# One set of raw token places for two groups, a half step with its transposes inside a product, and the last weight made in the last stage

## The chip, the core and the metric

The kernel runs on one core of one Trainium2 chip. A core has TensorE (PE, matrix products into PSUM, with its weight loads PEld beside them), VectorE (DVE), ScalarE (ACT), GpSimd (POOL) and SyncE (SP, which here issues most of the transfers). Each engine works through its own queue in order, and engines wait for each other by semaphores. The metric is the device time of one execution, in microseconds; the time of a kernel is the median of its runs.

## The reference

Three stages follow each other, all on 2304 tokens of 512 numbers:

```python
# 1. attention with a cumulative bias, 4 batches x 8 heads x 576 x 64
scores = scale * q @ k.T;  cum = cumsum(max(s, 0))
attn = softmax(where(causal, -1e9, scores + min(-(cum_i - cum_j), 0)))
x = attn @ v                               # 2304 x 512
# 2. mixture of 8 experts, each token to its best one
logits = x @ w_gate + modality_bias[modality_id];  e = argmax(logits)
x = prob[e] * (relu(x @ w1[e]) @ w2[e])    # F = 1024
# 3. gated projection, d_ff = 1536
out = (sigmoid(x @ w_gate2) * (x @ w_val)) @ w_out
```

The weights of stage 3 arrive as 64-bit numbers. The kernel makes 32-bit ones of them itself.

## The kernel before

**Order of work.** Everything is emitted by one program in one hand-made order, and each engine executes its part of it in that order. Attention runs a written period of steps over 16 pairs of heads. Between its steps `tick` takes one entry at a time from the router's queue `q` (an entry `None` lets a tick pass), and each batch of 576 tokens puts its routing steps there (`batch`, L622): the copy of the modality bias into the ninth column of the logits `lg` (POOL, L642), four empty ticks, their sum (L644), maximum, one-hot `oh` (L649), the entry `ranks` (small matmuls `rp`, L656 and L658, whose result is added into R at L653), the exponential, and the scatter of token numbers into a table. `lg` has two buffers, for batches of even and odd number.

**Expert stage.** When attention ends, `early` runs the first two slots of 256 tokens, 16 units; a unit is one eighth of the hidden size of one slot. It calls `main(u)` after each unit, which calls `router.pump(PUMPS[min(u, 3)])`: nine entries of the queue at unit 0, none at units 1 and 2, fourteen at each unit from 3 on. Unit 0's own products have already been emitted in attention; after `main(0)` come the products of unit 1. At unit 10 the table of tokens is transposed (`numbers`).

Then `run` (L1230) goes over units 16 to 71. In a unit, `mm1` makes twelve matmuls of 128x256, ScalarE writes the relu hH, VectorE the rest hL, and `mm2` of the unit before makes twelve more from hH and hL. After the unit `step(u)` emits what `todo` holds for it, and `aheads` splits the weights three units ahead (ScalarE `w`, then VectorE or POOL, L937 and L940) and loads the raw weights of the next slot. Unit numbers in `todo` are counted from 72 on: `put(-28, ...)` is unit 44.

After unit 71 come eight half steps (two half slots of 128 tokens, four steps each, `half`, L1129). A step transposes the hidden values of the step before (`half_t`, two matmuls L1111 and the VectorE copy hT, L1113), makes the first product (eight matmuls, L1134), has ScalarE write its relu, and then makes the second product of the step before (sixteen matmuls, L1122). `finish`, the last `mm2` of the slots, stands after the first half step.

**Filler work of the expert stage.** `Decode.stages` makes one piece of a 64-bit weight into 32 bits in four tasks: `near` (POOL, L877), `far` (VectorE, L881), `word` (ScalarE, L885) and `tail` (VectorE, L890), which also issues the next load. `last_weight` (L1290) does this for w_out, twelve pieces of 128x512 from unit 17 on, two units apart, and stores the results in DRAM as `wo32`. The eight pieces of the first gate and value weights (128x256 each) follow from unit 45 on, two units apart. `sums` (L1312) makes the seven sums of a token group that the fast product of stage 3 needs, in 18 tasks of 128x768: seven casts on ScalarE (L1317), seven rests (L1318) and four sums (L1319) on VectorE. Group 0 is loaded at unit 65 into four raw places `raws` and made at units 68 to 73, three tasks a unit. Group 1 has four raw places of its own (`raws1`), is loaded at unit 72 and made in units 74 to 79.

**Projection.** `Moe2.run` (L1662) goes over 36 units of seven slots. A slot is one product of six 128x384 matmuls per half (`product`, L1376); ScalarE takes a snapshot of a bank between two products into it (L1391), VectorE adds (L1403, L1410), ScalarE takes the sigmoid (L1405). Here too `todo` holds filler tasks by slot: group 2's sums up to slot 24, the pieces of the next weights (36 of them) in the slots from 12 on, and near the end the load of `wo32`. After that come the products with w_out.

The lines that order the filler work:

```python
for k, stages in enumerate(glu.last_weight(pool(wo_ctx, "dec", side="right", reuse_waits="tile"))):
    for i, task in enumerate(stages):
        put(2 * k + i - 55, [task])
...
put(-28, [wo_ctx.close, open_xs, glu.dec.load, glu.dec.load])
...
        put(2 * k + i - 27, [task])
...
put(-7, [lambda: glu.load_x(0, raws), lambda: glu.room_x(0, keep[0])])
```

Of the kernel before, what the change touches and what calls it, by code (L numbers as in the profile page):

```python
# [500 lines left out]
TROWS, PUMPS = 96, (9, 0, 0, 14)  # L501
# [5 lines left out]
class Router:  # L507
# [114 lines left out]
    def batch(self, b, xr, lg):  # L622
# [12 lines left out]
        tb = self.tb.rearrange("p (b t) e -> p b t e", t=5)[:, b]  # L635
# [36 lines left out]
        q.append(lambda: V.tensor_tensor(L, L, bc(mx), ALU.subtract))  # L672
        q.append(ranks)
# [174 lines left out]
class Decode:  # L848
# [7 lines left out]
    def __init__(self, tc, pool, n, srcs, bufs=2):  # L856
        self.nc, self.pool, self.srcs, self.size, self.bufs = tc.nc, pool, srcs, n, bufs
        self.raw, self.n, self.i = {}, 0, 0

    def load(self):  # L860

        if self.n < len(self.srcs):
            src = self.srcs[self.n]
            c, w = src.shape[1:]
            t = self.raw[self.n] = self.pool.tile([128, 8 * self.size], U8, tag="dr", name="dr", bufs=self.bufs)
# [3 lines left out]
    def stages(self, dst, then=None):  # L869

        nc, V, o, i, n = self.nc, self.nc.vector, {}, self.i, self.size
# [3 lines left out]
        def near():  # L875
            o["n"] = self.pool.tile([128, n], I8, tag="dn", name="dn", bufs=2)
            nc.gpsimd.tensor_scalar(o["n"], top(), 56.0, -56.0, ALU.min, ALU.max)  # L877

        def far():
            o["d"] = self.pool.tile([128, n], I8, tag="dd", name="dd", bufs=2)  # L880
# [17 lines left out]
class Moe:  # L898
    def __init__(self, tc, raw, ps, acc, router, w1, w2, x, x2, ids2, ident):
# [4 lines left out]
        self.prev, self.hprev, self.pend, self.ready = None, None, [], False  # L904
# [211 lines left out]
    def half_mm2(self, s, k, t):  # L1116
        nc = self.nc
        if k == 0:
            self.y[s] = [self.ps.tile([128, 512], F32, tag="tr", name="yh", bufs=BT)]
        for dc in range(4):  # L1120
# [5 lines left out]
        if k == 3:  # L1126
# [103 lines left out]
    def run(self, step):  # L1230
# [17 lines left out]
        ready = self.half_t(*self.hprev)  # L1248
        self.hprev = None
        self.half_mm2(*ready)  # L1250
# [7 lines left out]
class Moe2:  # L1258
# [10 lines left out]
    def __init__(self, tc, moe, x2, ids2, wg, wv, wo, out, hd, keep, rp, wo32):  # L1269
# [8 lines left out]
        self.dec = Decode(tc, keep, 256, srcs)  # L1278
# [11 lines left out]
    def last_weight(self, pool):  # L1290

        dec = Decode(self.tc, pool, 512, [self.wo[128 * f : 128 * f + 128, 3:].rearrange("(c p) b -> p c b", c=1) for f in range(12)], 3)
        for _ in range(3):
            dec.load()
        new = lambda: pool.tile([128, 512], F32, tag="dt", name="dt", bufs=2)
        return [dec.stages(new, lambda t, f=f: self.nc.sync.dma_start(self.wo32[128 * f : 128 * f + 128, :], t)) for f in range(12)]
# [365 lines left out]
    def run(self, ctx, rest):  # L1662
# [26 lines left out]
        spread(at(12, 0), at(15, 0), self.rows())  # L1689
        free = 0  # L1690
# [73 lines left out]
def kernel(ctx, tc, q, k, v, s, modality_id, moe_w_gate, modality_bias, w1, w2, wg, wv, wo, out):  # L1764
# [10 lines left out]
    with tc.manual_schedule():  # L1775
        ident = cp.tile([128, 128], F32, name="ident")
        make_identity(nc, ident)
        ps_ctx, at_ctx, mo_ctx, ea_ctx, mw_ctx, ex_ctx, xs_ctx, wo_ctx, x1_ctx = (ExitStack() for _ in range(9))
# [44 lines left out]
        def main(u):  # L1823
            if u >= 0:
                router.pump(PUMPS[min(u, 3)])
# [13 lines left out]
        todo, last, xs, raws, x1, raws1 = {}, 8 * MAIN, [], [], [], []  # L1839
# [99 lines left out]
```

## Time and profile before

| | us |
|---|---|
| median of three runs | 933.51 (931.78 to 933.62) |
| the profiled execution | 931.2 |
| its span, first to last instruction | 929.3 |
| TensorE busy | 890.6 (96%) |
| VectorE busy | 687.5 (74%) |
| ScalarE busy | 547.2 (59%) |
| POOL busy | 395.8 (43%) |
| granted TensorE clock, mean | 0.992 |

The span falls into attention (0 to about 250 us), the expert stage (to about 478), the half steps (to about 511) and the projection. Times of single instructions are counted from the start of the span. A matmul on full 32-bit operands appears as two records: the four of a half step's first product as eight, the eight of its second product as sixteen. Matmuls are pipelined, and their records overlap. Idle time is put down to the engine whose event came last before the start.

### The profile page before, as it was taken

How to read it: one execution, taken by the hardware profiler on the slowest of the kernel's cores; microseconds unless marked ns; L12 is line 12 of the kernel's file. 1: busy time of each engine (PE TensorE's matmuls, PEld its weight loads, DVE VectorE, ACT ScalarE, POOL GpSimd, SP SyncE). 2: the span in 40 equal slices, each digit the busy share in tenths (PEclk: the TensorE clock that was granted, in tenths of full speed). 3: DMA queues.
4: the chain of work that ended last, by engine and by line, in shares of the span. 5: the costliest groups of instructions: out<-in, count | busy, mean ns of one | idle time of the engine just before them, and what ended most of it. 6: DMA issues, size and time to landing. Idle time of an engine off the chain costs nothing. (4 is left out here: it accounts for less than half of the span.)

```text
span 929.3 us, 18666 instructions
## 1 busy us (share of the span) xinstructions
PE 890.6 (96%) x6261; PEld 856.7 (92%) x6261; DVE 687.5 (74%) x1549; ACT 547.2 (59%) x1282; POOL 395.8 (43%) x626
## 2 busy tenths in 40 slices
PE   7999999999889998999999999999999999999996
PEld 6898899898789998999998999999999998889996
DVE  5899999999765688867667766767575747868770
ACT  5999899898633656666544545354535345454440
POOL 7988889898822676776620001010000000111111
PEclk8999999999999999999999999999999999999998
DMA  6667659676314458523566422424242308573501
GB/s 170 155 146 177 142 94 141 154 146 225 97 22 80 143 176 262 193 92 92 178 211 215 114 81 80 139 78 136 74 139 68 116 18 300 153 225 110 170 35 45
DMA packets 163866, 125.29 MB, mean 135 GB/s; under 512 B 86737, under 2 KB 147692, under 8 KB 163254
## 3 DMA queue, kind: packets, MB, share of 16 engines
q1 hardware_dynamic: 158566, 112.44, 43.2%
q0 software_dynamic: 3984, 11.32, 4.3%
q8 instruction: 50, 0.82, 0.4%
q14 instruction: 50, 0.41, 0.2%
q10 hardware_dynamic: 1216, 0.30, 0.1%
HBM read 115.95 MB, written 33.23 MB: 161 GB/s over the span
## 5 line engine op out<-in xcount | busy, mean ns | idle before, releaser
L1382 PE MATMUL X<-a,set 128*128 128x384 f32 x864 | 164.1, 337 | 1.9 <-ACT u L1391 0.9
L1382 PEld LDWEIGHTS X<-a,set 128*128 128x128 f32 x864 | 151.7, 188 | 3.8 <-ACT u L1391 1.9
L877 POOL TENSOR_SCALAR dn<-dr 128x256 int8<-128x256 int8 (+1 forms) x60 | 34.4, 573 | 249.0 <-DMA dr<-in_moe_w_val_dram 91.3
L940 POOL TENSOR_TENSOR w<-raw,w 128x512 fp32r<-128x512 f32 x56 | 80.3, 1444 | 45.9 <-ACT w L937 43.6
L1519 POOL DMA_INDIRECT out_dram<-oy,row x18 | 20.2, 1120 | 167.5 <-ACT oy L1543 91.4
L175 POOL TENSOR_SCALAR bias<-cumB,cumT 128x576 f32<-128x576 f32 (+4 forms) x155 | 82.9, 537 | 19.3 <-DVE nm L294 18.3
L1004 PE MATMUL ph<-xT,w 128*128 128x256 f32 x672 | 88.6, 280 | 0.0
L1004 PEld LDWEIGHTS ph<-xT,w 128*128 128x128 f32 x672 | 82.4, 188 | 0.0
L1382 PE MATMUL Y<-a,set 128*128 128x384 f32 x432 | 81.5, 336 | 0.0
L303 ACT ACTIVATE P<-P,nm 128x576 f32<-128x576 f32 (+3 forms) x128 | 79.6, 628 | 0.6 <-DVE nm L294 0.6
L338 DVE TENSOR_TENSOR PL<-pt,PH 128x512 fp32r<-128x512 f32 (+1 forms) x128 | 76.9, 630 | 3.1 <-ACT PH L331 2.6
L1382 PEld LDWEIGHTS Y<-a,set 128*128 128x128 f32 x432 | 76.0, 188 | 0.1
L294 DVE CUSTOM_DVE_ANT_0 P<-sb,bias 128x320 f32<-128x320 f32 (+3 forms) x128 | 67.3, 550 | 6.4 <-PE sb L285 4.8
L1391 ACT COPY u<-X 128x384 f32<-128x384 f32 x72 | 34.5, 480 | 61.1 <-PE X L1382 61.0
L331 ACT CAST PH<-pt 128x512 fp32r<-128x512 f32 (+1 forms) x128 | 64.7, 551 | 5.8 <-PE pt L322 4.7
L322 PE MATMUL pt<-ident,P 128*128 128x128 f32 x448 | 64.1, 277 | 2.8 <-DVE QL L241 1.0
L1008 ACT ACTIVATE hH<-ph 128x256 fp32r<-128x256 f32 x72 | 27.7, 384 | 62.3 <-PE ph L1004 56.4
L940 DVE TENSOR_TENSOR w<-raw,w 128x512 fp32r<-128x512 f32 x56 | 54.7, 976 | 12.1 <-ACT w L937 11.4
L937 ACT CAST w<-raw 128x512 fp32r<-128x512 f32 x112 | 63.6, 619 | 0.0
L285 PE MATMUL sb<-KT,QH 128*128 128x288 f32 (+3 forms) x192 | 56.6, 319 | 4.7 <-DVE nm L294 4.2
L322 PEld LDWEIGHTS pt<-ident,P 128*128 128x128 f32 x448 | 51.6, 142 | 7.8 <-ACT P L303 3.2
L1317 ACT CAST hf<-hp 128x768 fp32r<-128x768 f32 x42 | 34.1, 835 | 38.9 <-DVE hp L1319 35.2
(317 smaller groups left out, 2393.2 us busy)
## 6 DMA issues: line engine op xcount, KB each, us to landing
raw<-in_moe_w_dram SPq DMA_DIRECT2D x80, 512.0 KB
h<-sg SPq DMA_DIRECT2D x72, 192.0 KB
cumB<-cum_d SPq DMA_DIRECT2D x32, 288.0 KB
hp<-h SPq DMA_DIRECT2D x24, 384.0 KB
qraw<-in_q_dram SPq DMA_DIRECT2D x58, 128.0 KB
dr<-in_moe_w_out_dram SPq DMA_DIRECT2D x12, 511.6 KB
dr<-in_moe_w_gate_dram SPq DMA_DIRECT2D x24, 255.2 KB
dr<-in_moe_w_val_dram SPq DMA_DIRECT2D x24, 255.2 KB
```

What stands on the lines that cost most here:

```text
L175: (nc.vector if n in FILLB else nc.gpsimd).tensor_scalar(res[i][:rows], cumB[:rows, :m], -1.0, self.cumT[:rows, i, n : n + 1], ALU.mult, A ...
L285: nc.tensor.matmul(self.sb[:rows, o : o + c1 - c0], X[:, T0[i] : T0[i] + rows], h["KT"][:, c0:c1], start=j == 0, stop=j == 1)
L294: nc.vector.tensor_tensor_reduce(out=pt[:rows, :m], in0=self.sb[:rows, o : o + m], in1=self.bias_t[n][i][:rows], op0=ALU.add, op1=ALU.min, ...
L303: nc.scalar.activation(h["P"][i][:rows, : T0[i] + rows], h["P"][i][:rows, : T0[i] + rows], AF.Exp, bias=h["nm", i][:rows], scale=-1.0, acc ...
L322: nc.tensor.transpose(pt[:, c : c + 128], h["P"][i][:, T0[j] : T0[j] + 128], self.ident)
L331: self.nc.scalar.copy(t[:, :z], pt[:, :z])
L338: self.nc.vector.tensor_tensor(t[:, :z], pt[:, :z], h["H"][u][:, :z].bitcast(F32), ALU.subtract)
L937: nc.scalar.copy(v, src)
L940: (eng or nc.vector).tensor_tensor(v, src, h.bitcast(F32), ALU.subtract)
L1004: nc.tensor.matmul(ph, w[:, 128 * dc : 128 * dc + 128], x[:, dc], start=k == 0, stop=k == 11)
L1382: self.nc.tensor.matmul(bank, w[:, c], a[:, h, c], start=first and k == 0, stop=k == 5, skip_group_check=True)
L1391: self.nc.scalar.copy(t, self.o[u, "X"])
```

## The change

Four things change together.

- The router's bias copy becomes `bias_in(b)`. It is made for the first two batches at set-up, and for batch b + 2 right after the sum of batch b. The four empty ticks ahead of the sum go. At unit 0 `pump` takes up to fourteen entries but stops ahead of the last batch's `ranks`; at units 1 and 2 it takes none, from unit 3 on fourteen.
- A half step transposes its own hidden values, after six of the eight matmuls (twelve of sixteen records) of the second product of the step before (`part=0`); the last two (`part=1`) follow the transposes. `half_end` then needs no transposes. In step 0 there is no second product yet, and the transposes follow the first product at once.
- w_out is made in the projection: 24 pieces of 128x256 instead of twelve of 128x512, 26/3 slots apart from slot 31 on, in places that group 2's raw values have left. The first gate and value weights take the room: their eight pieces are made from unit 24 on, four units apart.
- Group 0 is loaded at unit 54 and made one task at a time in units 56 to 70. Group 1 is loaded at unit 71 into the same raw places and made in units 73 to 80, two or three tasks a unit; the second set of places goes.

```diff
-TROWS, PUMPS = 96, (9, 0, 0, 14)
+TROWS, PUMP, RANKS = 96, 14, 3
+        for b in range(2):
+            self.bias_in(b)
+
+    def bias_in(self, b):
+        self.nc.gpsimd.tensor_copy(self.lg[b % 2][:, :, :, 8], self.tb.rearrange("p (b t) e -> p b t e", t=5)[:, b])
...
-        q.append(lambda: nc.gpsimd.tensor_copy(lg[:, :, :, 8], tb))
-        self.space(4)
         q.append(lambda: V.tensor_reduce(L.unsqueeze(3), lg, axis=AX.X, op=ALU.add))
+        if b + 2 < self.B:
+            q.append(lambda: self.bias_in(b + 2))
...
+        if b == self.B - 1:
+            self.last_ranks = ranks
         q.append(ranks)
...
-    def pump(self, n):
+    def pump(self, u):
         self.q = [f for f in self.q if f]
-        while self.q and n:
+        n = 0 if 0 < u < RANKS else PUMP
+        while self.q and n and (u or self.q[0] is not self.last_ranks):
...
     def half(self, s, k):
         nc = self.nc
-        ready = self.half_t(*self.hprev) if self.hprev else None
+        ready = self.hready
...
         if ready:
-            self.half_mm2(*ready)
-        self.hprev = (s, k, h)
+            self.half_mm2(*ready, part=0)
+        self.hready = self.half_t(s, k, h)
+        if ready:
+            self.half_mm2(*ready, part=1)

     def half_end(self):
-        self.half_mm2(*self.half_t(*self.hprev))
-        self.hprev = None
+        self.half_mm2(*self.hready)
+        self.hready = None
...
-    def last_weight(self, pool):
+    def last_weight(self):
...
+        raw = [self.ap.tile([128, 3072], U8, tag=f"xs{i}", name=f"dx{i}", bufs=1) for i in range(3)]
+        top = self.rp.tile([128, 4096], U8, tag="raw2_3", name="dx3", bufs=1)
+        dr = [raw[0][:, 0:2048], raw[1][:, 0:2048], top[:, 0:2048], top[:, 2048:4096]]
...
+        at = [(128 * f, 256 * l) for f in range(12) for l in range(2)]
...
+        def last_weight():
+            for k, stages in enumerate(self.last_weight()):
+                for i, task in enumerate(stages):
+                    put(at(4, 3) + 26 * k // 3 + i, [task])
+
+        put(at(3, 5), [last_weight])
...
-        for k, stages in enumerate(glu.last_weight(pool(wo_ctx, "dec", side="right", reuse_waits="tile"))):
-            for i, task in enumerate(stages):
-                put(2 * k + i - 55, [task])
...
-    put(-28, [wo_ctx.close, open_xs, glu.dec.load, glu.dec.load])
+    put(-49, [open_xs, glu.dec.load, glu.dec.load])
...
-            put(2 * k + i - 27, [task])
+            put(4 * k + i - 48, [task])
...
-    put(-7, [lambda: glu.load_x(0, raws), lambda: glu.room_x(0, keep[0])])
+    put(-18, [lambda: glu.load_x(0, raws), lambda: glu.room_x(0, keep[0])])
...
-        for k in range(6):
-            put(k - 4, x[3 * k : 3 * k + 3])
+        for k in range(18):
+            put(k * 5 // 6 - 16, [x[k]])
...
-        x, cuts = glu.x_tasks(1, raws1), (0, 3, 7, 9, 12, 15, 18, 18)
+        x, cuts = glu.x_tasks(1, raws), (0, 2, 4, 6, 9, 11, 13, 16, 18)
...
+    put(-1, [lambda: glu.load_x(1, raws)])
+    put(0, [later])
```

## Rows read from the trace of the kernel before

**Rows 1.** Waits of TensorE, whole span: line waited for, us in total, times, longest.

```profile
PE rp L656 <- DVE oh L649: 4.5, 1, 4.5
...
PE sb L1024 <- DVE hL L1009: 3.7, 4, 1.5
PE yh L1122 <- DVE hT L1113: 3.4, 3, 1.3
...
PE y L1024 <- DVE hL L1009: 1.9, 4, 0.9
```

**Rows 2.** Stretches: length, busy us (instructions) of each engine, clock, DMA share, GB/s.

```profile
320.00:383.00 63.00, 57.81 (x482) 56.39 (x481) 53.67 (x64) 38.12 (x78) 46.43 (x38) 1.00 0.68 221
383.00:430.00 47.00, 46.76 (x402) 46.56 (x402) 35.84 (x51) 30.11 (x65) 34.19 (x30) 1.00 0.29 92
...
478.00:512.00 34.00, 30.39 (x213) 27.81 (x211) 21.47 (x33) 13.66 (x26) 0.00 (x0) 1.00 0.59 195
512.00:545.00 33.00, 31.33 (x173) 29.96 (x174) 24.66 (x43) 19.15 (x39) 2.31 (x4) 1.00 0.39 113
545.00:775.00 230.00, 230.00 (x1316) 229.77 (x1316) 149.62 (x326) 105.83 (x235) 16.09 (x34) 1.00 0.30 99
```

**Rows 3.** TensorE in order of time, 252 to 265 us: start, us, line, shapes.

```profile
252.99 1.04 PE L988 MATMUL mtr<-ident,xg 128*128 128x128 f32 x8
258.50 0.20 PE L656 MATMUL rp<-oh,tri 128*128 128x48 bf16 x1 [4.48 <-DVE oh L649]
...
258.67 2.86 PE L1004 MATMUL ph<-xT,ew 128*128 128x256 f32 x12
...
263.12 1.60 PE L1004 MATMUL ph<-xT,ew 128*128 128x256 f32 x12
264.56 0.28 PE L1024 MATMUL y<-hH,ew 128*128 128x256 f32 x1
```

**Rows 4.** ScalarE and VectorE in order of time, 254 to 257 us.

```profile
254.94 1.07 ACT L993 CAST xT<-mtr 128x512 fp32r<-128x512 f32 x2 [2.60 <-PE mtr L988]
255.56 1.29 DVE L994 TENSOR_TENSOR xT<-mtr,xT 128x512 fp32r<-128x512 f32 x2 [1.50 <-ACT xT L993]
```

**Rows 5.** Stretches of one microsecond, PE first, granted clock third from the end.

```profile
240.00:241.00 1.00, 0.00 (x0) 0.00 (x0) 0.97 (x3) 1.00 (x3) 1.00 (x2) 1.00 0.86 324
...
259.00:260.00 1.00, 1.00 (x6) 1.00 (x6) 0.83 (x3) 0.00 (x0) 0.00 (x0) 0.50 0.00 0
```

**Rows 6.** TensorE, then VectorE, in order of time around one stop at 370 us.

```profile
368.20 0.28 PE L1024 MATMUL sb<-hH,w 128*128 128x256 f32 x1
370.00 0.39 PE L1024 MATMUL sb<-hL,w 128*128 128x256 f32 x1 [1.52 <-DVE hL L1009]
...
366.14 1.78 DVE L881 SCALAR_TENSOR_TENSOR dd<-dr,dn 128x512 int8<-128x512 int8 x1 [1.33 <-POOL dn L877]
367.84 1.77 DVE L940 TENSOR_TENSOR w<-raw,w 128x512 fp32r<-128x512 f32 x1
```

**Rows 7.** The tail step L890, two widths: minimum, median, maximum ns, first and last start.

```profile
L890 DVE SCALAR_TENSOR_TENSOR ds<-dr,ds x48: 407/418/1132, 407.6 to 737.5; 128x256 int32<-128x256 int32 x48
L890 DVE SCALAR_TENSOR_TENSOR dt<-dr,dt x12: 683/1360/3029, 320.5 to 390.0; 128x512 int32<-128x512 int32 x12
```

**Rows 8.** TensorE in order of time, the second half step.

```profile
479.08 1.89 PE L1134 MATMUL phh<-raw,xTh 128*128 128x256 f32 x8
482.24 2.05 PE L1122 MATMUL yh<-hT,raw 128*128 128x128 f32 x16 [1.27 <-DVE hT L1113]
```

**Rows 9.** VectorE, then ScalarE, in order of time, in the half steps.

```profile
480.90 0.96 DVE L1318 TENSOR_TENSOR a<-xs,a 128x768 fp32r<-128x768 f32 x1 [1.57 <-ACT a L1317]
481.77 0.42 DVE L1113 COPY hT<-hth 128x256 f32<-128x256 f32 x1
...
486.34 0.38 ACT L1136 ACTIVATE hh<-phh 128x256 f32<-128x256 f32 x1 [2.42 <-PE phh L1134]
```

**Rows 10.** The near step L877 in 540 to 780 us, minimum, median, maximum ns.

```profile
L877 POOL TENSOR_SCALAR dn<-dr x36: 405/412/807, 542.8 to 734.8; 128x256 int8<-128x256 int8 x36
```

More of the change, by code (lines that the diff above doesn't have):

```diff
@@ L848, with __init__, pool_room @@
 class Decode:
[L856 to L857 removed]
+    def __init__(self, tc, n, srcs, room):
+        self.nc, self.room, self.srcs, self.size = tc.nc, room, srcs, n
         self.raw, self.n, self.i = {}, 0, 0
+    @staticmethod
+    def pool_room(pool, n):
+        shapes = {"dr": ([128, 8 * n], U8), "dn": ([128, n], I8), "dd": ([128, n], I8)}
+        return lambda tag, i: pool.tile(*shapes[tag], tag=tag, name=tag, bufs=2)
     def load(self):
@@ L1114, in half_t, with half_mm2 @@
         return s, k, t
-    def half_mm2(self, s, k, t):
+    def half_mm2(self, s, k, t, part=None):
         nc = self.nc
-        if k == 0:
+        if k == 0 and part != 1:
             self.y[s] = [self.ps.tile([128, 512], F32, tag="tr", name="yh", bufs=BT)]
-        for dc in range(4):
+        for dc in range(4) if part is None else range(3) if part == 0 else range(3, 4):
             for j in range(2):
@@ L1125, in half_mm2 @@
                 )
-        if k == 3:
+        if k == 3 and part != 0:
             self.store(s)
@@ L1286, in preload @@
         self.nc.scalar.activation(t, t, AF.Sigmoid)
-    def last_weight(self, pool):
-        dec = Decode(self.tc, pool, 512, [self.wo[128 * f : 128 * f + 128, 3:].rearrange("(c p) b -> p c b", c=1) for f in range(12)], 3)
-        for _ in range(3):
+    def last_weight(self):
+        raw = [self.ap.tile([128, 3072], U8, tag=f"xs{i}", name=f"dx{i}", bufs=1) for i in range(3)]
+        top = self.rp.tile([128, 4096], U8, tag="raw2_3", name="dx3", bufs=1)
+        dr = [raw[0][:, 0:2048], raw[1][:, 0:2048], top[:, 0:2048], top[:, 2048:4096]]
+        cut = lambda a, n, k: raw[2][:, a + n * k : a + n * k + n]
+        places = {
+            "dr": dr, "dn": [cut(0, 256, k).bitcast(I8) for k in range(2)],
+            "dd": [cut(512, 256, k).bitcast(I8) for k in range(2)], "dt": [cut(1024, 1024, k).bitcast(F32) for k in range(2)],
+        }
+        room = lambda tag, i: places[tag][i % len(places[tag])]
+        at = [(128 * f, 256 * l) for f in range(12) for l in range(2)]
+        dec = Decode(self.tc, 256, [
+            self.wo[r : r + 128, 8 * c + 3 : 8 * c + 2048].rearrange("(c p) b -> p c b", c=1) for r, c in at
+        ], room)
+        for _ in range(4):
             dec.load()
-        new = lambda: pool.tile([128, 512], F32, tag="dt", name="dt", bufs=2)
-        return [dec.stages(new, lambda t, f=f: self.nc.sync.dma_start(self.wo32[128 * f : 128 * f + 128, :], t)) for f in range(12)]
+        store = lambda t, r, c: self.nc.sync.dma_start(self.wo32[r : r + 128, c : c + 256], t)
+        return [dec.stages(lambda k=k: room("dt", k), lambda t, r=r, c=c: store(t, r, c)) for k, (r, c) in enumerate(at)]
     def load_x(self, t, raws):
@@ L1777 @@
         make_identity(nc, ident)
-        ps_ctx, at_ctx, mo_ctx, ea_ctx, mw_ctx, ex_ctx, xs_ctx, wo_ctx, x1_ctx = (ExitStack() for _ in range(9))
+        ps_ctx, at_ctx, mo_ctx, ea_ctx, mw_ctx, ex_ctx, xs_ctx = (ExitStack() for _ in range(7))
         ps = pool(ps_ctx, "psum", space=PSUM)
@@ L1824, in main @@
             if u >= 0:
-                router.pump(PUMPS[min(u, 3)])
+                router.pump(u)
             if not router.q and phase[0] == 0:
@@ L1838 @@
         glu = Moe2(tc, moe, x2, ids2, wg, wv, wo, out, hd, keep[0], rp, wo32)
-        todo, last, xs, raws, x1, raws1 = {}, 8 * MAIN, [], [], [], []
+        todo, last, xs, raws = {}, 8 * MAIN, [], []
         def put(at, tasks):
@@ L1864, in open_second @@
             glu.room_x(1, glu.second)
-            x1.append(pool(x1_ctx, "x_second", side="right", reuse_waits="tile"))
-            raws1.extend(x1[0].tile([128, 2, glu.G], F32, name=f"xt{i}") for i in range(4))
-            glu.load_x(1, raws1)
         put(0, [open_second])
@@ L1891 @@
         moe.run(step)
-        x1_ctx.close()
         xs_ctx.close()
```

26 lines of the change are left out of this document (11 added, 15 removed).

## The prediction

> **What bounds the kernel now.** TensorE. I read the stretches first [rows 2]: in the token stage of the last projection (545 to 775 us) it is busy in every microsecond, while VectorE is busy in 149.6 of 230. So time can only be won where TensorE stops. The list of its waits says where [rows 1]: 4.5 us once for the router's one-hot (rp on oh, L649), 3.7 and 1.9 us in eight waits for hL in the expert slots, 3.4 us in three waits for hT in the half slots. The rest is attention (about 13 us in small pieces, not touched by more than a shift of ticks) and the first units of the projection (1.67 us idle in 512 to 545, [rows 2]). The change works on just these three places, so the question is how much of each goes, and what the moved work costs where it lands.
>
> A remark on idle time: a matmul record is longer than the distance to the next one, so the idle time of the profile is less than what is lost. Twelve starts from 263.12 to 264.56 lie 0.12 us apart, and the record of the twelve is 1.60 us, with a tail of 0.16 [rows 3]. At 368.20 a lone matmul started, its successor at 370.00 [rows 6]: 1.68 us were lost where the wait says 1.52. I add 0.16 us to each wait of this kind.
>
> **Part A, the router's last batch.** Before, `pump` at unit 0 takes nine entries, and the ninth puts the rank matmuls on TensorE ahead of unit 1. They wait for seven VectorE steps, which themselves stand behind the two xL steps of slot 1. TensorE stops at 254.03 (252.99 + 1.04) and resumes at 258.50 [rows 3]. After, unit 0 takes the VectorE steps alone, and the ranks come after unit 3. What is late next for unit 1 is its xT: the ScalarE halves run 254.94 to 256.01, the VectorE halves 255.56 to 256.85 [rows 4]. Those steps stand ahead of the router's and do not move. So product 1 of unit 1 can start on the first half at about 256.2 and must be free to run by 256.9. Then 1.44 us of mm1 and 1.44 us of mm2 (0.12 us each for 24) bring unit 2 to 259.1 to 259.8, against 263.12 [rows 3]: 3.3 to 4.0 us. The rank matmuls come back later, 0.17 us (258.50 to 258.67). That is 3.1 to 3.8 us.
>
> Part of this is clock. In 259 to 260 us the granted clock was 0.50, that is the 1.2 GHz level, after the stop of 4.5 us; the twelve matmuls at 258.67 took 2.86 us instead of 1.60 [rows 3, 5]. In 240 to 241 us, inside a stop of 1.6 us, it stayed at 1.00, the 2.4 GHz level [rows 5]. The new stop is 2.2 to 2.9 us, nearer to the second row, so I take full clock. If it falls all the same, the two products cost again the 1.57 us by which 258.67 to 263.12 exceeds 2.88, and 1.5 us are left. Value: 3.2 us, bounds 1.5 and 3.8. The ranks now come after unit 3's matmuls instead of before unit 1, so that scatter, table fetch and gather start about 0.8 us later against the units; the transposes of the table at unit 10 show no wait before, so I cost this at nothing (0 to 0.8 us if that cover is gone). On VectorE the add that reads the ranks now holds the queue at unit 3, and behind it stand only router steps and the split of a piece used two units later.
>
> The copies `bias_in` move two batches ahead, from POOL between attention's mask steps to the same queue elsewhere; the reductions come some five ticks earlier. No row prices that: between -1 and +1 us, taken as nothing.
>
> **Part B, the last weight leaves the expert stage.** Most of the waits for hL lie in 320 to 383 us, the stretch with the twelve 512-wide pieces; there TensorE is idle 5.2 us and VectorE busy 53.7 of 63. In 383 to 430, where the eight 256-wide pieces of the next weights are made at the same spacing of two units, TensorE is idle 0.24 us [rows 2]. One stall shows the mechanism: `far` of 1.78 us and a split of 1.77 us stand on VectorE ahead of hL, to 369.6, and the product goes on at 370.00 [rows 6]. The 512-wide `tail` took 1.36 us at the median and 3.03 at worst, the 256-wide one 0.42 [rows 7]. After, this stretch has no 512-wide piece, and the 256-wide pieces stand four units apart instead of two. The idle 5.2 us, and 0.16 us for each of at least five stops: 6.0 us. Bounds: 6.0, and 4.0 if a third of the stops is made by other steps. I take 6.0.
>
> **Part D, first token group over 15 units.** Eighteen tasks, eleven of them on VectorE (0.96 us each, [rows 9]), in units -16 to -2: 0.7 us of VectorE per unit of some 2.9 us. Before, the eight pieces in 383 to 430 loaded VectorE about as much (0.8 us per unit) and cost 0.24 us in all. Its load is issued two units ahead of the first task, where it was three. ScalarE would wait for it with a unit's relu behind. I take 0.3 us lost, bounds 0 and 1.5.
>
> **Part C, half steps.** Before, the transposes T of a half step stand at the head of the next one, and only its first product (eight matmuls, 1.89 us with tail) hides the VectorE copy hT. By about 480.8 the product of 479.08 is issued, and TensorE waits until 482.24, since hT starts at 481.77 behind a token task of 0.96 us [rows 8, 9]. Three such waits, 3.35 us by the profile and 0.17 more each: 3.9 us. After, T stands inside the second product: twelve of its sixteen matmuls (2.05 us for all, so 1.5) hide the relu of 0.38 us, the remaining four and the next first product (0.5 + 1.7) hide hT of 0.42. At most three VectorE tasks (2.9 us) fall into a step of some 4 us (1.89 + 2.05 and the transposes), and they are issued after the hT of their own step, so the next hT finds an empty queue. Two places stay open (with 0.1 us from one engine's end to the next one's start, where hT to TensorE shows 0.05, [rows 8, 9]). Step 0 has no second product before it: T waits for the relu with nothing between, 0.16 of tail + 0.1 + 0.38 + 0.1, about 0.74 us that `finish` covered before. The last hT has four matmuls as cover: 0.16 + 0.1 + 0.42 + 0.1 against 0.5 leaves 0.3 us. Net 3.9 - 1.1 = 2.8 us. Bounds 1.5 and 3.3: the second group's four loads now stand on SP a unit earlier, ahead of slot 8's store and the second half slot's weights, but they must wait for the last step of group 0; if they land late, the tasks of step 1 hold VectorE and ScalarE, and hT and the relu stand behind.
>
> **Part E, the last weight in the projection.** 24 pieces in 213 us: `near` 0.41 us on POOL, `far` and `tail` 0.42 us each on VectorE, `word` about as much on ScalarE [rows 7, 10]. That is 20 us of VectorE, which has 80 us idle in this stretch [rows 2]; the 36 pieces already there cost TensorE no wait. SP gets 24 loads and 24 stores among the stores of sg and the loads of the other weights; a weight that lands later holds `near`, and `far` holds VectorE. Bounds: 0, and 4 us if 0.17 us of each piece comes through. I take 0.7.
>
> Here the trace and a rule can be weighed. The 512-wide `tail` of 3.03 us ran while POOL worked, and the 256-wide ones, in a stage where POOL is busy 16 of 230 us, took 0.42 at the median [rows 2, 7]. The Trainium skill, SBUF — State Buffer, section "SBUF: two separate sides", says that a VectorE step with two inputs in SBUF and a GpSimd step shut each other out for a whole instruction. By that rule each added `near` could hold back one VectorE step by 0.41 us, 9.9 us of VectorE over the stage, still inside its idle time; the trace agrees in the expert stage, and no row here shows it for the projection.
>
> **The sum.** 3.2 + 6.0 - 0.3 + 2.8 - 0.7 = 11.0 us. The profiled execution took 931.2 us, 929.3 of it span, so it would be 920.2. It lies 2.3 us under the median of the three runs, 933.5, and the forecast for a median is 922.5.
>
> **Rivals.** (1) The projection gives much back: VectorE is full in some slots (its parts come in bursts), 0.2 us of each piece comes through, 4.8 us instead of 0.7: 926.6. For it: TensorE is idle 1.67 us in 512 to 545, where VectorE is busy 24.7 of 33 us; against it: none of the 36 pieces after 545 cost a stop. (2) The clock falls in the shorter stop: 1.7 us less, 924.2. For it 259 to 260, against it 240 to 241 [rows 5]. (3) The expert stage stalls in other places: the token steps and weight pieces are now spread over units that also split weights; half of B is made again: 925.5. For it: 0.96 us steps in a queue where 1.8 us too many stalled; against it 383 to 430 [rows 2]. (4) Slower: in the projection each piece holds VectorE by `far`, `tail` and a wait for `near`, 1.25 us together; ScalarE's sigmoid waits for VectorE's add, the next snap stands behind the sigmoid, and TensorE needs the snap for its X bank. When over 0.57 us of each piece reaches TensorE (13.7 us in 24), the gains of 11.7 and the 1.9 us of the noise are gone; at 0.65 it is 937. Against it: VectorE's 80 idle us. That the change doesn't take place at all as it says is part of (3).
>
> **How the numbers follow.** Forecast 0.54, (1) 0.15, (2) 0.12, (3) 0.11, (4) 0.05, and 0.03 for (1) and (3) together at their worst, within 1.9 us (0.2%, about what a measurement of this kernel can tell from no change) of the old time. Low end: all gains at their upper bounds, nothing given back, 919.5. High end: (1) with part of (2), 928. Faster 0.92, same 0.03, slower 0.05.
>
> **What would show it.** Right: no wait of rp on oh, and unit 1's products at about 256.5 at a granted clock of 1.00; no stop for hL in units 17 to 42; one stop of about 0.6 us at the first T and one of about 0.2 at the last hT; no idle TensorE in 545 to 775. Wrong: waits of X on the snaps u and p in that stage, relus held behind a token load near unit -16, or a clock of 0.50 after the router.

## The result, and the profile after

Six runs each on one chip: 924.36 us (922.26 to 925.17) after, 933.57 us (931.78 to 935.12) before, a ratio of 0.9897 with a 95% interval of 0.988 to 0.9914: 9.2 us less, where 11.0 were forecast, with the time inside the range. The profiled execution of after took 925.17 us (span 923.2), that of before 931.2: the slowest of its six and the fastest of its runs, so these two traces differ by 6.0 us only. The kernel after was profiled once more beside the last experiment (919.38 us, span 917.6); the ratio there was 0.990 (0.9872 to 0.9928).

TensorE's waits in the first profile of after (line waited for, us in total, times, longest), to be read beside [rows 1]. Lines moved: hL L1009 is now L1022, hT L1113 is L1126, hh is L1149, X L1382 is L1407 and its snaps are L1416.

```profile
PE X L1407 <- ACT u L1416: 2.7, 5, 1.2
PE y L1037 <- DVE hL L1022: 2.1, 1, 2.1
...
PE X L1407 <- ACTq L1103: 1.5, 1, 1.5
...
PE mtr L1001 <- DVE hL L1022: 0.9, 1, 0.9
...
PE hth L1124 <- ACT hh L1149: 0.5, 1, 0.5
...
PE ph L1017 <- DVE lg L409: 0.5, 1, 0.5
```

The wait for the one-hot (4.5 us), those for hT (3.4) and seven of the eight for hL are gone. In their place stand one wait for hL of 2.1 us, a branch wait (ACTq) that grew from 0.7 to 1.5, and more waits for the snap u in the projection.

The stretches of [rows 2], the first two 4 us earlier and the last 9, and one more from 426 us on that holds the first token group's tasks (length, busy us and instructions of PE, PEld, DVE, ACT, POOL, then clock, DMA share, GB/s):

```profile
316.00:379.00 63.00, 63.00 (x538) 63.00 (x538) 35.98 (x60) 39.55 (x85) 43.10 (x36) 1.00 0.43 138
379.00:426.00 47.00, 47.00 (x402) 47.00 (x402) 25.30 (x44) 28.72 (x61) 32.38 (x28) 1.00 0.32 102
426.00:470.00 44.00, 41.86 (x338) 41.52 (x337) 30.89 (x39) 22.63 (x46) 26.32 (x20) 0.96 0.45 140
...
536.00:769.00 233.00, 231.20 (x1315) 229.50 (x1314) 168.05 (x373) 113.65 (x259) 28.81 (x60) 1.00 0.42 135
```

The stretch of the 512-wide pieces has no idle TensorE now (5.2 us before). The one with the first token group has 2.1 us and a mean clock under 1.00, and the projection, where TensorE never stopped, has 1.8 us idle. Of the prediction's signs of being wrong this is the one that came: waits of X on the snap u.

**One table for all runs.** For each profile, the us between six points of TensorE: the starts of unit 0's twelve products, the first product of unit 16 and the first half step's product, the end of the last yh, and the starts of the projection's first X and the last stage's first acc. Each is a difference of two such times in that trace (before: 250.24, 304.73, 475.72, 511.74, 512.46, 777.42). The last stage took 151.4 to 152.6 us in all. The ratios are to runs of the kernel before on the same chip, whose medians lay between 929.9 and 935.0 us.

| run | unit 0 to 16 (A) | 16 to half steps (B, D) | half steps (C) | branch | projection (E) | median us | ratio to before (95%) |
|---|---|---|---|---|---|---|---|
| before | 54.49 | 170.99 | 36.02 | 0.72 | 264.96 | 933.57 | 1 |
| after | 50.57 | 167.52 | 32.95 | 1.45 | 268.21 | 924.36 | 0.9897 (0.988 to 0.9914) |
| after_again | 49.47 | 165.98 | 32.95 | 1.45 | 267.68 | 919.84 | 0.9900 (0.9872 to 0.9928) |
| a_router | 51.45 | 171.70 | 35.64 | 0.72 | 265.94 | 929.22 | 0.9935 (0.9912 to 0.9957) |
| a_ranks | 49.47 | 170.99 | 36.10 | 0.72 | 265.96 | 926.77 | 0.9965 (0.9951 to 0.9978) |
| c_half | 55.65 | 170.97 | 34.40 | 0.81 | 265.18 | 933.57 | 0.9979 (0.9958 to 1.0) |
| b_nodec | 55.16 | 164.51 | 35.66 | 0.72 | 265.13 | 927.77 | 0.9907 (0.9875 to 0.994) |
| d_shift | 52.51 | 165.91 | 32.96 | 1.45 | 267.84 | 923.47 | 0.9873 (0.9845 to 0.9902) |
| d_free | 49.46 | 164.42 | 33.36 | 1.68 | 269.61 | 920.07 | 0.9884 (0.9867 to 0.9902) |
| e_noload | 49.83 | 167.50 | 32.95 | 1.45 | 266.75 | 922.21 | 0.9904 (0.9889 to 0.9919) |
| e_nodec | 49.46 | 166.01 | 32.95 | 1.45 | 265.17 | 917.84 | 0.9867 (0.9843 to 0.9892) |
| best | 49.46 | 164.37 | 32.96 | 0.72 | 265.74 | 917.20 | 0.9858 (0.9831 to 0.9886) |

From the row before to after_again: 5.0 won in A, 5.0 in B and D, 3.1 in C; 0.7 lost at the branch and 2.7 in the projection. That is 9.7 us, about what the ratios say; to the first profile of after the same sum is 6.5. The projection of the five kernels with the old place of w_out took 264.96 to 265.96 us, with 1.1 to 1.2 us idle in each, so up to 1 us in that column is scatter.

### The profile page after: what moved, and what is told of

Same layout as the page of the kernel before. It is cut to its first block, busy times and chain, and to the rows that moved or that the text cites. A ratio compares the mean times of both kernels' runs of the same rounds, so it can differ in the third digit from the quotient of the medians.

```text
span 923.2 us, 18761 instructions
## 1 busy us (share of the span) xinstructions
PE 893.5 (97%) x6261; PEld 858.7 (93%) x6261; DVE 669.5 (73%) x1573; ACT 548.2 (59%) x1294; POOL 400.7 (43%) x638
## 5 line engine op out<-in xcount | busy, mean ns | idle before, releaser
L1407 PE MATMUL X<-a,set 128*128 128x384 f32 x864 | 164.8, 338 | 4.5 <-ACT u L1416 2.7
L1407 PEld LDWEIGHTS X<-a,set 128*128 128x128 f32 x864 | 151.6, 188 | 7.8 <-ACT u L1416 5.0
L890 POOL TENSOR_SCALAR dn<-dr 128x256 int8<-128x256 int8 x48 | 23.7, 496 | 226.5 <-DMA dr<-in_moe_w_val_dram 86.7
L953 POOL TENSOR_TENSOR w<-raw,w 128x512 fp32r<-128x512 f32 x56 | 82.8, 1486 | 51.6 <-ACT w L950 42.1
L175 POOL TENSOR_SCALAR bias<-cumB,cumT 128x576 f32<-128x576 f32 (+4 forms) x155 | 82.9, 537 | 12.9 <-DVE nm L294 12.1
L1407 PE MATMUL Y<-a,set 128*128 128x384 f32 x432 | 81.5, 336 | 0.0
L1407 PEld LDWEIGHTS Y<-a,set 128*128 128x128 f32 x432 | 76.0, 188 | 0.1
L1022 DVE SCALAR_TENSOR_TENSOR hL<-ph,hH 128x256 fp32r<-128x256 f32 x72 | 30.4, 422 | 45.9 <-ACT hH L1021 44.5
L953 DVE TENSOR_TENSOR w<-raw,w 128x512 fp32r<-128x512 f32 x56 | 49.8, 889 | 18.0 <-ACT w L950 17.4
L1416 ACT COPY u<-X 128x384 f32<-128x384 f32 x72 | 34.4, 478 | 46.2 <-PE X L1407 45.9
```

Of the source, the lines that this page charges most:

```text
L175: (nc.vector if n in FILLB else nc.gpsimd).tensor_scalar(res[i][:rows], cumB[:rows, :m], -1.0, self.cumT[:rows, i, n : n + 1], ALU.mult, A ...
L953: (eng or nc.vector).tensor_tensor(v, src, h.bitcast(F32), ALU.subtract)
L1407: self.nc.tensor.matmul(bank, w[:, c], a[:, h, c], start=first and k == 0, stop=k == 5, skip_group_check=True)
```

## The experiments

**The router alone (a_router), and half of it (a_ranks).** The edit of the second; the first moves the bias copies as well:

```diff
+        if b == self.B - 1:
+            self.last_ranks = ranks
...
-    def pump(self, n):
+    def pump(self, u):
         self.q = [f for f in self.q if f]
-        while self.q and n:
+        n = 0 if 0 < u < RANKS else PUMP
+        while self.q and n and (u or self.q[0] is not self.last_ranks):
```

> The kernel before with part A alone (the last router batch: its vector steps at unit 0, its rank matmuls after unit 3, the bias copies two batches ahead). Theory: the 4.5 us wait of TensorE for the one-hot (rp on oh) is gone, what is left at unit 1 is a wait of 2 to 3 us for its xT, and unit 2's product starts near 259.4 us of the span instead of 263.1; nothing is given back later, so the time is 3.5 to 4.2 us under before. Rival, the clock: after the shorter stop TensorE runs at 1.2 GHz all the same, and only 1.5 to 2 us are won. Rival, the table: the ranks come after unit 3, so the gathers come later and TensorE stops for the table or for xT near unit 10 to 16; then the gain at unit 2 is 4 us and the time is within 2 us of before.

> The kernel before with the first half of part A alone: the last batch's rank matmuls after unit 3, the bias copies where they were. With both halves the time was 929.2 where before was at 935.0, while from unit 0's product to unit 2's only 3 us are won. Theory (attention's length scatters from run to run by several us whatever the bias copies do; its medians differ by chance): the time is within 1 us of the kernel with both halves, unit 2 starts 8.7 to 10.4 us after unit 0, before 12.9. Rival (the bias copies on GpSimd in the middle of attention cost 2 to 3 us): the same 8.7 to 10.4 us there, but the time is 2 to 3 us above the kernel with both halves, about 932 us for 935 of before.

TensorE in order of time at unit 1 in a_router (start, us, line, tiles, idle before and who ended it), against [rows 3]:

```profile
246.84 1.69 PE L1012 MATMUL ph<-xT,ew 128*128 128x256 f32 x12
252.55 0.39 PE L1012 MATMUL ph<-xT,ew 128*128 128x256 f32 x1 [1.92 <-ACT xT L1001]
253.28 1.58 PE L1012 MATMUL ph<-xT,ew 128*128 128x256 f32 x11 [0.34 <-DVE xT L1002]
256.14 1.60 PE L1012 MATMUL ph<-xT,ew 128*128 128x256 f32 x12
```

Unit 2 comes 9.3 us after unit 0 (12.9 before), with xT as what is late next and a clock of 1.00. The same place in a_ranks has waits of 0.2 and 0.3 us, and unit 2 comes 7.6 us after unit 0, less than the 8.7 to 10.4 expected. Two things made the difference, and neither follows the code: with the router of the whole change unit 2 came after 7.6, 8.7 or 10.4 us. The first is when ScalarE reads the transposes: 0.64 us after their start in a_ranks (250.26, 250.90), 2.32 in a_router (249.59, 251.91), 1.95 in before (252.99, 254.94). On one chip ScalarE was late at this place by 1.2 us or more in all four profiles, on two others in none of six; the trace doesn't show what it waits for. (In c_half and in the first profile of after it was late one step sooner, at unit 0's relu, by 1.9 and 1.7 us. In after the transposes then stop for 0.9 us, the wait of mtr above, and unit 2 comes after 8.7 us.) The second is the clock: in d_shift a stop of 2.0 us at this place was followed by a granted clock of 0.50 (1.2 GHz) from 256 to 259 us, and unit 2 came after 10.4 us; in a_router, with 1.9 us, it stayed at 1.00 (2.4 GHz).

By the ratios a_router wins 6.1 us (4.0 to 8.2), more than the 3.5 to 4.2 expected, and a_ranks 3.3 (2.0 to 4.6). Whether the bias copies matter for attention is not settled. The two ratios, 0.9935 and 0.9965, would allow 2.8 us between the two kernels, but they are from two chips and their intervals touch; unit 0 starts at 247.5 us of the span without the move (a_ranks) and at 246.8 with it, the third and the first of all twelve profiles.

**The half steps alone (c_half).**

```diff
-        ready = self.half_t(*self.hprev) if self.hprev else None
+        ready = self.hready
...
-            self.half_mm2(*ready)
-        self.hprev = (s, k, h)
+            self.half_mm2(*ready, part=0)
+        self.hready = self.half_t(s, k, h)
+        if ready:
+            self.half_mm2(*ready, part=1)
```

> The kernel before with part C alone (in a half step the transposes of h stand inside the second product). Theory: the three waits for hT (3.4 us) are gone, a first wait of about 0.5 us for hh stays, and the way from the first half-step product to the last yh (36.0 us before) is 2.8 to 3.1 us shorter; the time is 2.8 to 3.1 us under before. Rival: the token tasks on VectorE, which the waits for hT had room for, come late instead and stop TensorE in the second group's products or at the branch of the projection; then the hT waits are gone and the time is within 1.5 us of before.

The waits for hT are gone, but only 1.2 to 1.7 us are won of the 3.1 that the whole change wins here, where 2.8 to 3.1 were expected. TensorE, then ScalarE, in order of time at the fourth half step:

```profile
496.59 1.50 PE L1122 MATMUL yh<-hT,raw 128*128 128x128 f32 x12
499.02 0.44 PE L1111 MATMUL hth<-ident,hh 128*128 128x128 f32 x2 [0.93 <-ACT hh L1136]
```

```profile
496.39 0.83 ACT L1317 CAST a<-xt 128x768 fp32r<-128x768 f32 x1 [3.33 <-DMA xt<-x]
497.85 0.83 ACT L1317 CAST a<-xt 128x768 fp32r<-128x768 f32 x1 [0.62 <-DMA xt<-x]
498.59 0.38 ACT L1136 ACTIVATE hh<-phh 128x256 f32<-128x256 f32 x1
```

The relu hh stands behind token casts that wait for their load; a second stop of 0.84 us at 485.27 has group 0's casts ahead of the relu. So the rest of C's gain comes from the last part of the change (D): in after, group 0's tasks are no longer in the half steps, group 1's load is issued a unit earlier and no relu stands behind a cast that waits for it, and the sole stop left is the 0.5 us at the first T.

**Without the 512-wide pieces (b_nodec).** The arithmetic goes; loads and stores stay, with a constant tile, `still`, in place of the result:

```diff
-        return [dec.stages(new, lambda t, f=f: self.nc.sync.dma_start(self.wo32[128 * f : 128 * f + 128, :], t)) for f in range(12)]
...
+        def moves(f):
+            dec.raw.pop(f)
+            dec.load()
+            self.nc.sync.dma_start(self.wo32[128 * f : 128 * f + 128, :], still)
...
+        return [[nothing, nothing, nothing, lambda f=f: moves(f)] for f in range(12)]
```

> The kernel before without the arithmetic of the twelve 512-wide pieces of the last weight in the expert stage (none of their four steps runs, on any engine; their loads and stores stay, a constant tile is stored, so the second output's projection weights are not those of the reference). Theory: it is the vector time of these steps that stops TensorE: the stops for hL between 320 and 383 us go from 5.2 us of idle TensorE to under 0.7, and the first half-step product starts 5.5 to 7.5 us earlier than in before (475.7). Rival (the transfers of these pieces delay the experts' weights or the gathers): the stops stay at 3 us or more, and the start moves by less than 3 us.

The stretch of [rows 2] in this kernel, 5 us later:

```profile
325.00:388.00 63.00, 63.00 (x538) 63.00 (x538) 32.11 (x51) 38.17 (x80) 39.87 (x32) 1.00 0.69 227
```

TensorE doesn't stop, with the transfers still there (227 GB/s, 221 before): it was the arithmetic. By the waits for hL and [rows 6] that is VectorE's steps; the run takes out ScalarE's and GpSimd's too, and how much of it is GpSimd holding VectorE isn't told apart. From unit 16 to the half steps it took 164.51 us against 170.97 to 171.70 with the pieces: B is worth 6.5 to 7.2 us.

**The first token group dealt otherwise (d_shift, d_free).** In after, unit 61 has two of its tasks; d_shift rounds so that it has one, d_free leaves units 60 and 61 free:

```diff
-            for k in range(18):
-                put(k * 5 // 6 - 16, [x[k]])
+                put((5 * k + 2) // 6 - 16, [x[k]])
...
+            for k, u in enumerate((56, 57, 58, 58, 59, 62, 62, 63, 63, 64, 65, 65, 66, 67, 67, 68, 69, 70)):
+                put(u - last, [x[k]])
```

> The kernel after, with the eighteen tasks of the first token group dealt to the same units by another rounding: the units that get two tasks are 58, 63 and 68 instead of 56, 61 and 66 (the xT transposes of a slot and a split of gathered weights stand in unit 61). Theory (a coincidence in one unit): the stop of 2.14 us for hL near 440 us and the 3 us at a granted clock of 0.50 behind it are gone, no stop of over 0.6 us takes their place between 430 and 465 us, and the first half-step product starts 2.5 to 4 us earlier than in after (468.8): 920.5 to 922 us where after is at 924.4. Rival (VectorE is short of time in the whole stretch, since token tasks run into GpSimd): a stop of 1 to 2 us for hL appears in another of the three units and the time stays within 1 us of after.

> The kernel after with two changes of dealing. First, the eighteen tasks of the first token group leave units 60 and 61 free (where GpSimd splits gathered weights and VectorE's steps with two inputs take 1.8 to 2.1 us instead of 0.7 to 0.95) and stand in 56 to 59 and 62 to 70. Theory (VectorE is full in just these two units): no stop of TensorE over 0.6 us between 430 and 465 us, and the way from the first gathered product of unit 16 to the first half step is 164.0 to 165.0 us, where after has 167.5, the kernel dealt by another rounding 165.9, and the one before without the last weight's arithmetic 164.5. Rival (the whole stretch is short of VectorE): a stop of 1 us or more in units 62 to 70, and 165.5 us or more. Second, nothing of the second token group is left for step 8, where ScalarE reads the branch. Theory: the wait of TensorE at the branch goes back from 1.45 to 0.7 us. Rival (the branch waits for the copy of yt itself): it stays over 1.2. Time if both theories hold: 920 to 921.5 us.

What made the stop in after: TensorE, VectorE and GpSimd in order of time.

```profile
442.77 0.54 PE L1037 MATMUL y<-hL,w 128*128 128x256 f32 x1 [2.14 <-DVE hL L1022]
```

```profile
437.78 0.94 DVE L1343 TENSOR_TENSOR a<-xs,a 128x768 fp32r<-128x768 f32 x1
438.65 2.06 DVE L1344 TENSOR_TENSOR xs<-xs,xs 128x768 f32<-128x768 f32 x1
440.63 1.75 DVE L953 TENSOR_TENSOR w<-raw,w 128x512 fp32r<-128x512 f32 x1
442.30 0.41 DVE L1022 SCALAR_TENSOR_TENSOR hL<-ph,hH 128x256 fp32r<-128x256 f32 x1
442.64 0.94 DVE L1344 TENSOR_TENSOR xs<-xs,xs 128x768 f32<-128x768 f32 x1
443.50 0.68 DVE L953 TENSOR_TENSOR w<-raw,w 128x512 fp32r<-128x512 f32 x1
```

```profile
438.06 3.77 POOL L953 TENSOR_TENSOR w<-raw,w 128x512 fp32r<-128x512 f32 x2 [1.68 <-ACT w L950]
```

Two token tasks and a split stand ahead of hL, and while GpSimd splits weights (438.06 to 441.83) a token step takes 2.06 us and VectorE's split 1.75; right behind it the same two take 0.94 and 0.68. The trace agrees here with the rule of the Trainium skill, SBUF — State Buffer, section "SBUF: two separate sides", that a VectorE step with two inputs in SBUF and a GpSimd step that reads SBUF shut each other out.

In d_shift a stop of 1.55 us for hL stayed at the same place (441.63), now with one token task of 2.09 and the split of 1.77 ahead of it: the coincidence of two tasks was only part of it, the rival was half right. With the units free (d_free) no stop over 0.5 us is left, and the way is 164.42 us, as without any last weight in b_nodec.

The clock behind this stop is a cost of its own. The same stop, in the two profiles of the same kernel (stretches of one microsecond; the clock is third from the end); first after, then after_again, where TensorE resumed at 439.21 behind a wait of 2.13:

```profile
443.00:444.00 1.00, 1.00 (x6) 1.00 (x7) 1.00 (x2) 0.39 (x1) 0.00 (x0) 0.50 0.00 0
444.00:445.00 1.00, 1.00 (x6) 1.00 (x6) 0.52 (x2) 1.00 (x3) 0.00 (x0) 0.50 0.00 0
```

```profile
440.00:441.00 1.00, 1.00 (x11) 1.00 (x10) 0.96 (x3) 0.94 (x2) 0.00 (x0) 1.00 0.00 0
441.00:442.00 1.00, 1.00 (x11) 1.00 (x10) 0.55 (x1) 0.94 (x2) 0.00 (x0) 1.00 0.13 22
```

With the clock at 0.50 the way was 167.52 and 167.50 us (after, e_noload), at 1.00 it was 165.98 and 166.01 (after_again, e_nodec): 1.5 us. So D costs 1.6 us by its stop, and 3.1 where the clock falls behind it.

The second edit of d_free, no token task in step 8, failed. ScalarE, then TensorE, at the branch in d_free:

```profile
500.20 0.83 ACT L1342 CAST a<-xs 128x768 fp32r<-128x768 f32 x1 [2.81 <-DVE xs L1344]
500.94 0.58 ACT L1050 COPY yt<-yh 128x512 f32<-128x512 f32 x1
```

```profile
501.62 1.32 PE L1407 MATMUL X<-a,set 128*128 128x384 f32 x6 [1.68 <-ACTq L1103]
```

In after a cast of 0.83 us stood between yt and the branch. Now four tasks in step 7 put it ahead of yt, where it waits for VectorE. The clock was at 0.50 from 504 to 506 behind this stop, and the projection of d_free is 1.4 us longer than that of after.

**The 24 pieces in the projection (e_noload, e_nodec).** The first leaves out the loads of pieces 5 to 24, the second the arithmetic:

```diff
+        def keep():
+            if dec.n < 24:
+                dec.raw[dec.n] = room("dr", dec.n)
+                dec.n += 1
+
+        dec.load = keep
```

```diff
-        return [dec.stages(lambda k=k: room("dt", k), lambda t, r=r, c=c: store(t, r, c)) for k, (r, c) in enumerate(at)]
+        return [[nothing, nothing, nothing, lambda k=k, r=r, c=c: moves(k, r, c)] for k, (r, c) in enumerate(at)]
```

As in b_nodec, `moves` keeps the load and stores a constant tile, so that no store waits for a piece.

> The kernel after without the loads of the last weight's pieces 5 to 24 in the projection (their arithmetic and their stores stay and work on the raw bytes of the first four, so the projection weight of the last stage isn't the reference's, nor what hangs on it). From the projection's first product to the first of the last stage the kernel after took 268.2 us, the four kernels with the old place of this weight 265.0 to 265.9. Theory (transfers: a piece's load lands behind those of the other weights, near waits for it on GpSimd, far on VectorE, and the snaps behind): most of the cost goes, 265.3 to 266.3 us, and the stop of 1.2 us for the snap u near 563 us is gone. Rival (the arithmetic itself delays the snaps): 267.5 to 268.5 us, the stop stays.

> The kernel after without the arithmetic of the last weight's 24 pieces in the projection (none of their four steps runs; all loads and stores stay, a constant tile is stored, so the projection weight of the last stage is zero and its output isn't the reference's). Theory (transfers): the late loads still delay the other weights' pieces, so more than half of the 3 us stays: 266.8 us or more from the projection's first product to the last stage's first, if near of the other pieces waits for loads that come late. Rival (the steps on GpSimd, VectorE and ScalarE are what delays the snaps): 265 to 266 us and no stop at 563 us. If both this kernel and the one without loads come to 265.5, it is the wait of these steps for their own loads.

265.17 us without the arithmetic, as with the old place of the weight: the theory of transfers fell there, since all loads stayed. 266.75 without the loads, between the two forecasts: 0.9 to 1.5 us of the 2.7 to 3.2 come back (against the profile of before), and the stop at 563 is gone. The two meet in SP's queue. SP in order of time in after, then GpSimd, then TensorE, and at the end SP and GpSimd at the same place in before:

```profile
551.26 0.33 SPq L879 DMA_DIRECT2D dx<-in_moe_w_out_dram  x1
551.65 0.42 SPq L1320 DMA_DIRECT2D wo<-dx  x1
552.12 0.42 SPq L1438 DMA_DIRECT2D h<-sg  x1
552.66 0.96 SPq L879 DMA_DIRECT2D dr<-in_moe_w_val_dram  x2
```

```profile
558.25 0.41 POOL L890 TENSOR_SCALAR dn<-dr 128x256 int8<-128x256 int8 x1 [18.66 <-DMA dr<-in_moe_w_val_dram]
```

```profile
563.03 1.14 PE L1407 MATMUL X<-a,set 128*128 128x384 f32 x5 [1.20 <-ACT u L1416]
```

```profile
560.20 1.38 SPq L866 DMA_DIRECT2D dr<-in_moe_w_val_dram  x2
...
562.93 0.78 POOL L877 TENSOR_SCALAR dn<-dr 128x256 int8<-128x256 int8 x1 [19.09 <-DVE u L1410]
```

The new load and store wait on SP, behind VectorE's steps on their piece, until 551.26, and the loads of the other weight stand behind them: issued 49.5 us after the projection's first X (47.7 before, 47.8 in e_nodec), and near starts 5.6 us after their issue (2.7 before, 2.8 in e_nodec). In e_noload, where the store alone stands ahead of them, they are issued after 48.8 us and near starts 2.9 us behind; why they land so late in after isn't shown. Then pieces of both weights come at once on VectorE, and the snap u behind them. The stops at 629.64 and 718.88 (0.2 and 0.4 us) stay without the loads and go without the arithmetic: there, steps of a piece and the parts of another weight share a slot on VectorE.

**A better dealing (best), and the kernel after beside it (after_again).** The free units of d_free, the second group with two tasks in step 7 and none in step 8, and the pieces at slots of their own:

```diff
+            ticks = (31, 44, 51, 63, 70, 82, 89, 101, 108, 121, 128, 142, 149, 163, 170, 184, 191, 205, 212, 222, 225, 228, 231, 234)
...
-                    put(at(4, 3) + 26 * k // 3 + i, [task])
+                    put(ticks[k] + i, [task])
...
-            x, cuts = glu.x_tasks(1, raws), (0, 2, 4, 6, 9, 11, 13, 16, 18)
+            x, cuts = glu.x_tasks(1, raws), (0, 2, 5, 9, 11, 14, 16, 18, 18)
```

> The kernel after once more, beside the next one on the same chip. Theory (what differs between profiles of the same code is when ScalarE reads unit 1's transposes and whether TensorE's clock falls behind a stop of 1.5 to 2.5 us): the stop for hL near 440 us is there again with 2.1 us; the way from the first gathered product of unit 16 to the first half step is 167.5 us if the granted clock is 0.50 behind it and 166.0 if it stays at 1.00; unit 2 starts 7.6 us after unit 0 if ScalarE starts the xT at once, 8.7 to 10.4 if late. Rival (these differences come from the edits of the other kernels): the values of the first profile, 167.5 and 8.7, come again with a clock of 1.00 or with xT in time. Median 0.988 to 0.991 of before.

> The kernel after with three changes of dealing: the first token group leaves units 60 and 61 free; the second token group has two tasks, not four, in step 7 and none in step 8; the 24 pieces of the last weight in the projection start at slots in which VectorE has no task of another weight two slots later. Theory: from the first gathered product of unit 16 to the first half step 164.0 to 165.0 us (after 167.5); TensorE's wait at the branch 0.7 to 0.9 us instead of 1.45 (the copy yt is neither behind nor ahead of a token task on ScalarE); from the projection's first product to the last stage's first 265.2 to 266.5 us (after 268.2), no stop of over 0.5 us there after 545. Together 4.5 to 7 us less than after: a ratio to before of 0.982 to 0.985. Rival (the steps of the 24 pieces cost TensorE something wherever they stand, and the twelve that now come late in the projection, close together, make stops of their own there): 267 us or more in the projection, and a ratio of 0.986 or more.

All three places came out as the theory had them: 164.37 us, 0.72 and 265.74. TensorE's waits in best:

```profile
PE X L1407 <- ACT u L1416: 1.3, 3, 0.5
...
PE sb L1037 <- DVE hL L1022: 0.8, 2, 0.5
PE X L1407 <- ACTq L1103: 0.7, 1, 0.7
```

The projection still does 24 pieces with the same loads, so most of what they cost in after (1.9 to 2.5 us) was their place, not their work. From unit 0 to the end best takes 665.3 us, after_again 669.4, before 679.1. The medians on that chip are 917.20 us (915.29 to 919.18) and 919.84 (919.24 to 923.46) for 929.93 of before: 2.6 us, less than the 4.1 of the traces. The forecast of 4.5 to 7 us was reckoned from the first profile of after, in which the clock fell (7.2 us from unit 0 on), and by the medians it was missed: the ratio of 0.9858 lies at the rival's end while its mechanism doesn't show. Attention scatters by more than this difference. best has the lowest ratio of the kernels that compute everything, though the intervals of d_shift and d_free overlap with its own.

## Why the prediction was right, and where its steps were wrong

The sum, 11.0 us, was near by luck in part, because errors of both signs were in it: by the profiles 5.0 (A) + 5.0 (B and D) + 3.1 (C) - 0.7 (branch) - 2.7 (E) = 9.7. The low end of the range, 919.5, goes beyond its own terms: 3.8 + 6.0 + 3.3 = 13.1 us give 920.4, and 919.4 only with the 1 us allowed for the bias copies.

- **A, 3.2 us forecast, 5.0 between the profiles of before and after_again, 3.3 by the ratio of a_ranks (2.0 to 4.6).** The mechanism held: no wait for the one-hot, xT late next, full clock at unit 1 in both profiles of after. The step that failed is "those steps stand ahead of the router's and do not move": in the profile of before ScalarE read the transposes 1.3 us later than it does in six other profiles, so part of what was taken for fixed differs between executions. No profile has the old router with ScalarE in time, so A's size isn't pinned down better than this. The rival of the clock was seen at this place in d_shift (unit 2 after 10.4 us), and not in the two profiles of after.
- **B, 6.0 forecast, 6.5 to 7.2.** Right in mechanism and nearly in size; the upper bound was 0.5 to 1.2 too low. The term that was too small is the number of stops: the sum had five tails of 0.16 us, where the trace of before has nine stops for hL between unit 16 and the half steps, 5.7 us and 7.1 with the tails, against 0.8 in b_nodec. That is 6.3 of the 6.5; in the three other profiles with the old place the stops leave 1.2 to 1.6 us unexplained.
- **C, 2.8 forecast, 3.1.** Right, with the 0.5 us at the first T; the 0.3 at the last hT did not come. The working didn't say that half of the gain hangs on D: alone it is 1.2 to 1.7.
- **D, 0.3 lost forecast, bounds 0 and 1.5; 1.6 by its stop and 3.1 with the clock.** For its size the term that was most in error. Its working took 0.7 us of VectorE per unit against 0.8 in 383 to 430, a mean over units; the queue of one unit decided, with two tasks in it, and the price of 0.96 us was taken from the half steps, where GpSimd is idle (0.00 busy, [rows 2]), while the same step takes 2.06 beside its splits. The 0.8 is too high as well: in 383 to 430 the pieces' steps on VectorE took 10.8 us, 0.67 per unit, and five of the eight pieces had their `far` there. The trace of before already had a token step beside a split (VectorE, then GpSimd):

```profile
469.17 1.55 DVE L1318 TENSOR_TENSOR a<-xs,a 128x768 fp32r<-128x768 f32 x1
...
468.60 1.31 POOL L940 TENSOR_TENSOR w<-raw,w 128x512 fp32r<-128x512 f32 x1 [2.99 <-ACT w L937]
```

- **The branch, not in the sum, 0.7 lost.** The second group's tasks were looked at as a load on hT; that its last cast now stands between yt and the branch on ScalarE was overlooked.
- **E, 0.7 lost forecast, bounds 0 and 4; 2.7 to 3.2 against the profile of before, 1.7 to 3.3 against all five with the old place.** Rival (1) in kind, at about half its price: most of it is made in three slots, not by 0.2 us of each piece. The prediction named SP's 24 loads and 24 stores and a late load that holds near; it didn't see that a store waiting for its piece would itself hold the other weight's loads.

Rival (4) did not come: the kernel is faster. Of (3) one unit came true, as D; between 316 and 426 us TensorE has no idle time.

## What to carry to other kernels

Where work is moved into a stage with idle time, look at the queue of each engine unit by unit, not at the mean: all three losses here were single places where two things met, and moving tasks by a few units took most of them away. Price a VectorE step by a row in which GpSimd does what it will do beside it. A store put on the queue that also issues loads passed its wait on to them here: they were issued 1.8 us later.

## What was not expected of the hardware

The same stop of 2.1 us in the same code was followed by a granted clock of 0.50 in two profiles and of 1.00 in two others, and stops of 1.9 and 2.0 us at unit 1 likewise (a_router 1.00, d_shift 0.50). Behind the stop of 2.1 us the fall cost 1.5 us, and no row read here tells which it will be.

Attention, with the same arithmetic in all, ended between 246.8 and 255.9 us. In c_half and b_nodec 4.2 us of it, against before, came from one place, a stop and a clock of 0.50 behind it: VectorE, in order of time in c_half.

```profile
74.97 0.18 DVE L589 CAST fill<-mi 128x20 f32<-128x20 int32 x1 [2.10 <-DMA x<-fill]
75.18 1.39 DVE L591 TENSOR_SCALAR fill<-fill 128x20 f32<-128x20 f32 x1
```

The step overwrites a tile that by the profile a transfer (two parts of 512 KB) still reads, and TensorE stands 4.0 us behind it (in e_nodec, after a wait of 1.8 us, 2.4). In the other nine profiles the transfer was done in time, in before too. So two profiles can differ by 4 us far from the edit, and starts counted from unit 0 told more here than spans.
